# Sparse attention and a dropless mixture of experts: three row gathers one step earlier, a second layer 2 in another PSUM bank, one tile weighed by two engines

## The chip, the cores and the metric

The kernel runs on one core of one Trainium2 chip. The metric is the time of the launch in device microseconds, as a median of several runs. The core has five engines with an instruction stream each: TensorE (PE in the profile, its weight loads PEld), VectorE (DVE), ScalarE (ACT), GpSimd (POOL) and SyncE (SP). They wait for each other by semaphores. Sixteen DMA engines move data; in this kernel SP issues the plain transfers (queue q1) and GpSimd the indirect ones, which take their row numbers from a tile (queue q0).

## The reference

Attention comes first. There are 4 batches, 8 heads, 768 positions and a head dimension of 64. A block of 32 queries sees its own and the neighbouring key blocks, the first and last block, and three sampled blocks; the first and last query blocks see everything. Then each of the 3,072 rows of 512 numbers goes to one of 8 experts:

```python
logits = x @ w_gate
expert_idx = np.argmax(logits, axis=1)
...
for e in range(E):
    lo, hi = (boundaries[e], boundaries[e + 1])
    ...
    h = np.maximum(x_sorted[lo:hi] @ w1[e], 0.0)
    y_sorted[lo:hi] = h @ w2[e]
y = y_sorted[inv_perm]
return (gate_w[:, None] * y).astype(np.float32)
```

w1 is 512 x 1,024 and w2 is 1,024 x 512 for each expert, all in float32; gate_w is the softmax weight of the chosen expert.

## The kernel before

**Attention** is a list of 48 steps (`steps`): four batches, six groups of 128 queries, and two halves of the heads for each. In a step TensorE makes the scores of that step, ScalarE takes their exponential (L361), VectorE masks them (L367), and TensorE multiplies the *previous* step's exponentials with the values (`attend`, L385), in three chunks of the keys. The values that the queries see lie in the tile `around`, in two sets; GpSimd fetches them from `v_rows` with indirect transfers (`fetch_values`, L519), one to three steps ahead. `not_before` (L533) is a copy of one number on GpSimd: it waits for another engine's result, so that the fetches behind it are not issued too soon. In steps of an even place the fetch `fetch_values(b, g, 1, 1)` fills what the third chunk of `attend` reads in the next step. `divide` writes the rows x to `x_rows` in DRAM, `logits` makes their expert scores.

The order of the work on TensorE, VectorE and GpSimd is that of the code (`manual_schedule`); in attention this holds for ScalarE and SP too.

**Routing** is done twice. The rows of the first two batches (A) are sorted while attention still runs on the last two, and fill the first KA = 5 tiles of 128 rows; their row numbers (`gA`) are ready in the fourth-last step. The other tiles (B) are laid out after attention.

**The experts** run over NS = 18 tiles in a loop, with tile i + 1 in layer 1 while tile i is in layer 2. A tile takes these steps:

- `gather(i)` (L1048): GpSimd fetches the tile's 128 rows, 520 numbers each, from `x_rows` into one of four `xg` tiles. Column 512 is gate_w.
- `turn_x(i)`: the rows are transposed, on TensorE (L1119) for tiles 0 to 3 and on VectorE (L1111) after that.
- `layer1(i)` (L1130): two halves g of 16 matmuls each into a PSUM tile `hp`. ScalarE's relu (L1137) empties each half; what is handed in as `between` (the next tile's `turn_x`, or `turn_h`) stands between the halves in TensorE's order.
- `layer2_pe(i)` (L1144): eight matmuls of 512 columns into a PSUM tile of 512 numbers for each partition, which is one bank.
- `weigh(i)` (L1149): ScalarE multiplies the bank with gate_w on its way to SBUF.
- `put` (L1159): GpSimd writes the rows to their places in the output.

Before the loop, tile 0 is turned ahead of attention's last `attend`, and its `layer1` follows with `turn_out_late` (L476) and `turn_x(1)` between the halves.

Three **units** (at tiles 8, 11 and 14, `AT`) take an expert's last two tiles, one of them filled in part, as one wide tile of 128 to 224 columns (`layers_u`, L1248, L1256, L1265), inside a `Switch` over the width. A unit stands together with the layer 2 of two ordinary tiles, i before it and i + 1 behind it. It takes five PSUM banks: `banks[0]` and `banks[1]` from the pool `ps_h`, whose two buffers `layer1` uses also, `banks[2]` and `banks[3]` from the pool `ps_m`, and one from `ps_z`. After a unit comes a **small** tile of 32 rows (`layer1_s` L1198, `turn_h` L1207, `layer2_s` L1215; PSUM from `ps_m`), interleaved with the next tile's `layer1`.

Behind the loop a `Switch` over the number `arm` runs as many further tiles as the data needs beyond NS, with the same `layer1`, `layer2` and `weigh`. SP fetches the expert weights, 2 MB for each layer of a tile, three places ahead into buffers that TensorE has left.

Of the kernel before, what the change touches and what calls it, by code (L numbers as in the profile page):

```python
# [11 lines left out]
AF = mybir.ActivationFunctionType  # L12
# [5 lines left out]
def kernel(  # L18
# [11 lines left out]
    nc = tc.nc  # L30
# [8 lines left out]
    N, DM = out.shape  # L39
# [18 lines left out]
    NS = KA - -(N - KA * P - KU * MW - KS * QS) // P  # L58
# [5 lines left out]
    scale = 1.0 / float(D) ** 0.5  # L64
# [244 lines left out]
    def parity(b, g):  # L309
        return (b * NG + order.index(g)) % 2  # L310
# [220 lines left out]
    def not_before(at):  # L531

        nc.gpsimd.tensor_copy(paced[:], at)  # L533
# [489 lines left out]
    st = [{} for _ in range(NC)]  # L1023
# [22 lines left out]
    def gather(i):  # L1046
        xg = st[i]["xg"] = keep_xg[i % 4]
        nc.gpsimd.indirect_dma_start(  # L1048
            out=xg[:], out_offset=None, in_=x_d[: TA * P, :] if i < KA else x_d[:, :], in_offset=bass.IndirectOffsetOnAxis(ap=of("g", i, P), axis=0),
        )  # L1050
# [91 lines left out]
    def layer2_pe(i, zp):  # L1142
        for fb in range(FB):
            nc.tensor.matmul(  # L1144
                zp[:], lhsT=st[i]["hT"][:, fb, :], rhs=st[i]["w2"][:, fb, :], start=(fb == 0), stop=(fb == FB - 1),
            )

    def weigh(i, zo, zp):
        nc.scalar.activation(zo, zp[:], AF.Copy, scale=st[i]["xg"][:, DM : DM + 1])  # L1149

    def layer2(i, group):
        zp = upper["ps_z"].tile([P, DM], F32, name="zp")
# [157 lines left out]
    for i, (b, g, half) in enumerate(steps):  # L1310
        here = i % (2 * NG)
        prs = (2 * half, 2 * half + 1)
        nxt = steps[i + 2] if i + 2 < len(steps) else None

        if nxt is not None:
            b_, g_, half_ = nxt
            if half_ == 0:
                place_middle(b_, g_)
        if half == 0 and i > 0 and len(tiles_of(g)) > 1:
            if nxt is not None:  # L1320
                not_before(xk[0:1, parity(*nxt[:2]), 0, D : D + 1])
            fetch_values(b, g, 1, 1)
        if nxt is not None and half_ < len(tiles_of(g_)):
            place_keys(b_, g_, half_, on_vector=1 if b_ == B - 1 else NR)
        two = half == 1 and i + 1 < len(steps) and len(tiles_of(steps[i + 1][1])) > 1
        if two:
            b_, g_, _ = steps[i + 1]
            not_before(kr[0:1, parity(b_, g_), 1, 0, NKR - 1 : NKR])
            fetch_values(b_, g_, 1, 0)

        if g == GL:
            plans = [plan_all(b, pr) for pr in prs if b > 0] + [plan_two(b, prs)]
            *e_alls, e = scores(*plans)
            masked_two(e)
            mine = [(b, g, pr, e_alls[pr % 2] if b > 0 else None, e) for pr in prs]
        else:
            found = scores(*[plan(b, g, pr) for pr in prs])
            for e in found:
                masked(e, g)
            mine = [(b, g, pr, None, e) for pr, e in zip(prs, found)]  # L1340
        late = here + 2 * NG * (b - B + 2)
        for what in PARTS.get(late, ()):
            fetch_part(*what)
        if half == 1 and i + 1 < len(steps):
            not_before(mine[1][4][0:1, 0, 0:1])
            fetch_values(*steps[i + 1][:2], 0, 1)

        copy_turned = None
        if b + 1 < B:
            if b == 0 and here < 2:  # L1350
                fill_next(1, 2 * here)
                fill_next(1, 2 * here + 1)
            if 2 <= here < 10:
                copy_turned = turn(b + 1, (here - 2) // 2, here % 2, None, (here - 2) // 2 % 2)
                if here < 6:
                    fill_next(b + 1, here + 2)
        if b + 2 < B and here >= 8:
            fill_next(b + 2, here - 8)

        out_of = steps[i - 3][:2] if i >= 3 and half == 1 else None  # L1360
        if copy_turned:
            copy_turned()
        if i > 0 and before[0][1] != GL:
            attend(before, (lambda: turn_out(*out_of)) if out_of else None)
        elif i > 0:
            for n, (b_, g_, pr, e_all, e) in enumerate(before):
                attend_last(b_, pr, e_all, e)
                if n == 0 and out_of:
                    turn_out(*out_of)
        if "gates" in rt:  # L1370
            gate_weights()
        if out_of:
            logits(*out_of)
            if out_of[1] == order[-1]:
                gate(out_of[0])
        if i > 0:
            divide(*steps[i - 1])
        early(late)
        if half == 0 and nxt is not None:
            if i >= 2:  # L1380
                fetch_ends(*nxt[:2])
                b_, g_, half_ = steps[i - 1]
                not_before(sums[0:1, b_ * NG + g_, 4 * half_ : 4 * half_ + 1])
            fetch_values(*nxt[:2], 0, 0)
        if half == 1 and nxt is not None:
            place_values(*nxt[:2])
        if b + 1 < B:
            load_v(b + 1, V_AT[b > 0].get(here, ()))
            if 7 <= here < 10:
                keep_v(b + 1, (2 * here - 14, 2 * here - 13))  # L1390
        if 3 <= i < 11:
            route_consts(i - 3)
        if i == 11:
            route_tokens()
        if i == len(steps) - 2:
            gather(0)
        if i == len(steps) - 1:
            not_before(mine[1][4][0:1, 0, 0:1])
            gather(1)
        before = mine  # L1400
    turn_x(0)
    attend(before)
    divide(*steps[-1])
    gather(2)
    attn_by_hand.close()
    fetch(2, 1)
    fetch(2, 2)
# [7 lines left out]
    for i in range(NS):  # L1415
        if i == 0:
            ranks("B", TA, NT)
        if i + 3 <= NS + 1:
            gather(i + 3)
        here = AT_S.index(i) if i in AT_S else None  # L1420
        if here is not None:
            layer1_s(here)
            fetch_after(("small", here), 1)
        if i + 1 < NS:
            layer1(i + 1, lambda: turn_x(i + 2), *([turn_h] if here is not None else []))
            fetch_after(i + 1, 1)
        if here is not None:
            layer2_s(here)
            fetch_after(("small", here), 2)

            layer2(i + 1, "rows_out")
            fetch_after(i + 1, 2)
            leave_s(here, "rows_out")
        if i == 0:
            count("B")
            layout_b()
        if i + 3 in AT:
            gather_u(AT.index(i + 3))
        if i + 3 in AT_S:
            gather_s(AT_S.index(i + 3))  # L1440
        if i + 2 in AT:
            turn_u()
        if i + 2 in AT_S:
            turn_s()
        if i in AT or i - 1 in AT:

            continue
        if i + 1 in AT:


            u = AT.index(i + 1)
            zps = [upper["ps_z"].tile([P, DM], F32, name="zp") for _ in range(2)]
            zos = [next_of("z", keep_z) for _ in range(2)]
            banks = [upper["ps_h"].tile([P, DM], F32, name="hpu", tag="hp") for _ in range(2)]
            banks += [upper["ps_m"].tile([P, DM], F32, name="tpu", tag="tpg") for _ in range(2)] + zps[1:]
            layer2_pe(i, zps[0])
            fetch_after(i, 2)
            for more in tc.Switch(index[u], QR // STEP + 1):
                weigh(i, zos[0], zps[0])
                layers_u(u, P + more * STEP, banks)  # L1460
                layer2_pe(i + 1, banks[1])
                weigh(i + 1, zos[1], banks[1])
            fetch_after(("unit", u), 1)
            fetch_after(("unit", u), 2)
            fetch_after(i + 1, 2)
            put(of("s", i, P), zos[0], "rows_out")
            leave_u(u, "rows_out")
            put(of("s", i + 1, P), zos[1], "rows_out")
            continue
        layer2(i, "rows_out")  # L1470
        fetch_after(i, 2)
        if i == 1:
            tokens("B", NT, NB_)
        if i == 2:
            judge()
        if i == 4:
            tokens_s()
        if i == 3:
            for u in range(KU):
                at = rt["xeU"][0:1, KU + u : KU + u + 1]  # L1480
                index[u] = {
                    mybir.EngineType.PE: nc.tensor.value_load(at, min_val=0, max_val=QR // STEP),
                    mybir.EngineType.Activation: nc.scalar.value_load(at, min_val=0, max_val=QR // STEP),
                }
# [93 lines left out]
```

## Time and profile before

| | before |
|---|---|
| median of 3 runs | 640.75 us (636.26 to 643.61) |
| the profiled execution | 641.06 us |
| its span in the profile | 639.4 us |
| TensorE busy | 611.1 us (96%) |
| VectorE, ScalarE, GpSimd busy | 305.4, 230.6, 189.2 us |
| mean granted TensorE clock | 0.973 |
| DMA | 170.94 MB, mean 267 GB/s |

The profile shows one execution. Its page gives the busy time of each engine, the span in 40 slices (PEclk is the granted TensorE clock in tenths, DMA the share of the DMA engines' time), the costliest groups of instructions by line of the kernel, and the transfers. Other views list the instructions of one engine in order of time, the waits by who waited for whom, and the instructions of one tile. A bracket such as [1.75 <-DMA xg<-x_rows,gA] says that the engine sat idle for 1.75 us and that the landing of this transfer ended it. "paced" is what `not_before` writes.

### The profile page before, as it was taken

The numbers are of one execution on the slowest core, as the hardware profiler recorded it, in microseconds if no ns is written. First come the engines' busy times: TensorE is split into PE (matmuls) and PEld (weight loads), VectorE is DVE, ScalarE is ACT, GpSimd is POOL, SyncE is SP. The second block draws the span as 40 slices with busy tenths as digits, with TensorE's granted clock in tenths as the row PEclk, the third lists the DMA queues.
The fourth block names the chain that finished last, engine by engine and source line by source line (L and its number), as shares of the span: only waits on it lengthen the run. The fifth ranks groups of instructions, "written<-read, shape, count | busy, mean of one in ns | idle before, by whom it ended". The sixth has DMA issues, their size and how long they took to land. (4 is left out here: it accounts for less than half of the span.)

```text
span 639.4 us, 21377 instructions
## 1 busy us (share of the span) xinstructions
PE 611.1 (96%) x8938; PEld 512.6 (80%) x8938; DVE 305.4 (48%) x980; ACT 230.6 (36%) x456; POOL 189.2 (30%) x289
## 2 busy tenths in 40 slices
PE   7998989999999999989999999999999999999994
PEld 7898888889998989987777777877878787966862
DVE  7546665765578647725952485303091208303300
ACT  5546755774577758721111011111111111111110
POOL 2245844552366336720112221011401140020110
PEclk8869999997999989999999999999999999999998
DMA  8889977896797748899988999879997999669710
GB/s 266 210 182 233 238 195 165 205 244 180 162 209 202 240 141 260 261 344 339 345 306 315 336 387 351 289 234 385 397 399 281 370 398 399 260 220 408 281 39 19
DMA packets 125066, 170.94 MB, mean 267 GB/s; under 512 B 71236, under 2 KB 71237, under 8 KB 124934
## 3 DMA queue, kind: packets, MB, share of 16 engines
q1 hardware_dynamic: 114896, 137.61, 66.2%
q0 software_dynamic: 10000, 31.59, 15.9%
q8 instruction: 80, 1.31, 0.9%
q14 instruction: 52, 0.43, 0.2%
q10 hardware_dynamic: 38, 0.00, 0.0%
HBM read 150.11 MB, written 19.33 MB: 265 GB/s over the span
## 5 line engine op out<-in xcount | busy, mean ns | idle before, releaser
L1111 DVE STREAM_TRANSPOSE around<-xg 32x128 f32<-32x128 f32 x240 | 72.6, 303 | 121.9 <-PE hp L1130 92.7
L519 POOL DMA_INDIRECT around<-v_rows,rows_of x88 | 99.7, 1133 | 59.3 <-issue 23.4
L361 ACT ACTIVATE ea<-s 128x768 f32<-128x768 f32 x104 | 79.8, 809 | 78.4 <-PE s L356 66.7
L1130 PEld LDWEIGHTS hp<-around,room 128*128 128x128 f32 x832 | 94.5, 192 | 4.3 <-issue 2.7
L385 PE MATMUL op<-around,ea 128*64 128x65 f32 x2112 | 90.5, 229 | 7.3 <-DMA around<-v_rows,rows_of 6.1
L1130 PE MATMUL hp<-around,room 128*128 128x128 f32 x832 | 96.4, 276 | 0.9 <-ACT kr L1137 0.9
L385 PEld LDWEIGHTS op<-around,ea 128*64 128x64 f32 x2112 | 78.8, 141 | 16.1 <-DMA around<-v_rows,rows_of 7.4
L367 DVE TENSOR_TENSOR ea<-ea,mask 128x768 f32<-128x768 f32 x80 | 73.2, 954 | 20.0 <-ACT ea L361 19.1
L1144 PE MATMUL zp<-room,kr 128*128 128x512 f32 x176 | 77.6, 594 | 0.0
L1137 ACT ACTIVATE kr<-hp 128x512 f32<-128x512 f32 x36 | 21.5, 597 | 117.1 <-PE hp L1130 109.1
L1144 PEld LDWEIGHTS zp<-room,kr 128*128 128x128 f32 x176 | 32.6, 190 | 37.2 <-issue 37.2
L1159 POOL DMA_INDIRECT out_dram<-kr,sB x14 | 14.1, 1008 | 161.3 <-ACT kr L1149 106.0
L1149 ACT ACTIVATE kr<-zp,xg 128x512 f32<-128x512 f32 x16 | 11.0, 687 | 101.2 <-PE zp L1144 101.2
L1130 PEld LDWEIGHTS hp<-around,other 128*128 128x128 f32 x384 | 43.8, 192 | 3.0 <-issue 2.3
L1130 PE MATMUL hp<-around,other 128*128 128x128 f32 x384 | 44.4, 276 | 0.5 <-ACT kr L1137 0.5
L1237 DVE STREAM_TRANSPOSE ea<-ea 32x128 f32<-32x128 f32 x84 | 21.7, 285 | 32.6 <-DMA ea<-x_rows,gB 31.9
L1144 PE MATMUL zp<-other,kr 128*128 128x512 f32 x80 | 35.3, 593 | 0.0
L1144 PEld LDWEIGHTS zp<-other,kr 128*128 128x128 f32 x80 | 14.9, 190 | 17.4 <-issue 17.4
L356 PE MATMUL s<-other,kr 64*128 64x64 f32 x352 | 27.0, 266 | 1.2 <-issue 1.2
L356 PE MATMUL s<-room,kr 64*128 64x64 f32 x352 | 26.7, 266 | 0.5 <-issue 0.5
L1159 POOL DMA_INDIRECT out_dram<-kr,sA x5 | 5.1, 1024 | 73.9 <-ACT kr L1149 73.9
L356 PEld LDWEIGHTS s<-other,kr 64*128 64x128 f32 x352 | 25.3, 195 | 1.2 <-issue 1.2
(362 smaller groups left out, 945.0 us busy)
## 6 DMA issues: line engine op xcount, KB each, us to landing
room<-in_moe_w_dram SPq DMA_DIRECT2D x30, 2048.0 KB
other<-in_moe_w_dram SPq DMA_DIRECT2D x16, 2048.0 KB
room<-in_moe_w_dram SPq DMA_DIRECT2D x16, 512.0 KB
x_rows<-xb SPq DMA_DIRECT2D x20, 256.0 KB
room<-in_k_dram SPq DMA_DIRECT2D x24, 192.0 KB
room<-in_q_dram SPq DMA_DIRECT2D x24, 192.0 KB
v_rows<-room SPq DMA_DIRECT2D x12, 260.0 KB
v_rows<-other SPq DMA_DIRECT2D x12, 260.0 KB
```

What stands on the lines that cost most here:

```text
L356: nc.tensor.matmul(s[:, hh, a : a + n], lhsT=keys(r), rhs=queries(r), start=True, stop=True)
L361: nc.scalar.activation(e, s[:, :, : 6 * D], AF.Exp, scale=scale)
L367: nc.vector.tensor_tensor(e, e, m[:, None, :].to_broadcast([P, 2, 6 * D]), op=ALU.mult)
L385: nc.tensor.matmul(op[ti * D : (ti + 1) * D, pr % 2, hh, : D + 1], lhsT=e, rhs=values[:, (2 * pr + hh) * VW : (2 * pr + hh + 1) * VW], sta ...
L519: nc.gpsimd.indirect_dma_start(out=around[p0:, par, 1 + ti + 2 * ch, :], out_offset=None, in_=v_d[b][:, :], in_offset=bass.IndirectOffsetO ...
L1111: nc.vector.transpose(xT[d, :, t], xg[t, :DM].rearrange("p (c q) -> p c q", c=DB)[:, :, d])
L1130: nc.tensor.matmul(hp[:, m, :], lhsT=st[i]["w1"][:, c, fb * P : (fb + 1) * P], rhs=st[i]["xT"][:, c, :], start=(c == 0), stop=(c == DB - 1),)
L1137: nc.scalar.activation(hT[:, g * (FB // 2) : (g + 1) * (FB // 2), :], hp[:], AF.Relu)
L1144: nc.tensor.matmul(zp[:], lhsT=st[i]["hT"][:, fb, :], rhs=st[i]["w2"][:, fb, :], start=(fb == 0), stop=(fb == FB - 1),)
L1149: nc.scalar.activation(zo, zp[:], AF.Copy, scale=st[i]["xg"][:, DM : DM + 1])
L1159: ins = nc.gpsimd.indirect_dma_start(out=to[:, :], out_offset=bass.IndirectOffsetOnAxis(ap=at, axis=0), in_=rows, in_offset=None, bounds_c ...
L1237: nc.vector.transpose(xT_u[d, :, j * P + tq * 32 : j * P + (tq + 1) * 32], xg_u[t, j, :DM].rearrange("p (c q) -> p c q", c=DB)[:, :, d],)
```

## The change

Three edits.

1. gather(0), gather(1) and gather(2) are issued at the ends of attention's last three steps, in place of the ends of the last two and the place behind the last `divide`. The `not_before` of the last step now stands ahead of gather(2), where it stood ahead of gather(1).
2. Inside a unit, the layer 2 of tile i + 1 goes to `banks[3]`, from the pool `ps_m`, in place of `banks[1]`, from `ps_h`.
3. For tile NS - 1 = 17, `weigh` is cut into two halves of 256 columns: VectorE takes the upper, ScalarE the lower one. Every other tile's `weigh` stays as it was.

```diff
     def weigh(i, zo, zp):
-        nc.scalar.activation(zo, zp[:], AF.Copy, scale=st[i]["xg"][:, DM : DM + 1])
+        of_i = st[i]["xg"][:, DM : DM + 1]
+        if i == NS - 1:
+            nc.vector.tensor_scalar_mul(zo[:, DM // 2 :], zp[:, DM // 2 :], of_i)
+            nc.scalar.activation(zo[:, : DM // 2], zp[:, : DM // 2], AF.Copy, scale=of_i)
+            return
+        nc.scalar.activation(zo, zp[:], AF.Copy, scale=of_i)
...
             route_tokens()
-        if i == len(steps) - 2:
-            gather(0)
-        if i == len(steps) - 1:
-            not_before(mine[1][4][0:1, 0, 0:1])
-            gather(1)
+        if i >= len(steps) - 3:
+            if i == len(steps) - 1:
+                not_before(mine[1][4][0:1, 0, 0:1])
+            gather(i - len(steps) + 3)
         before = mine
     turn_x(0)
     attend(before)
     divide(*steps[-1])
-    gather(2)
     attn_by_hand.close()
...
                 layers_u(u, P + more * STEP, banks)
-                layer2_pe(i + 1, banks[1])
-                weigh(i + 1, zos[1], banks[1])
+                layer2_pe(i + 1, banks[3])
+                weigh(i + 1, zos[1], banks[3])
```

## The prediction

> **What bounds it now.** I read the page first, then TensorE's order of time where the change sits, then the waits. The page:
>
> ```profile
> span 639.4 us, 21377 instructions
> PE 611.1 (96%) x8938; PEld 512.6 (80%) x8938; DVE 305.4 (48%) x980; ACT 230.6 (36%) x456; POOL 189.2 (30%) x289
> PEclk8869999997999989999999999999999999999998
> ```
>
> TensorE is busy for 611.1 of 639.4 us. The page's chain of waits holds only the last 1.3 us (the last write's issue), so it doesn't lead back into the kernel; TensorE's own gaps do, and I added them up from the matmuls' starts and ends: 18.6 us in all before the last matmul, most of it in attention. A change that neither cuts matmuls nor moves the clock can win only such a gap, or the tail behind the last matmul. From 240 us to the tail the stretches at half clock are over (table of windows: PEclk 1.00 in each), so a gap that closes there is worth its own length.
>
> Two kinds of gap lie under this change. The first is where attention ends; TensorE in order of time, the bracket telling an idle time and what ended it:
>
> ```profile
> 274.72 1.35 PE L385 MATMUL op<-around,ea 128*64 128x65 f32 x31
> ...
> 276.47 0.66 PE L1119 MATMUL tp<-ident,xg 128*128 128x128 f32 x4
> 277.06 1.62 PE L385 MATMUL op<-around,ea 128*64 128x65 f32 x48
> 278.61 3.84 PE L1130 MATMUL hp<-around,room 128*128 128x128 f32 x32
> 282.29 0.60 PE L476 MATMUL xrl<-ident,xb 128*128 128x128 f32 x4
> 284.63 0.66 PE L1119 MATMUL tpg<-ident,xg 128*128 128x128 f32 x4 [1.75 <-DMA xg<-x_rows,gA]
> ```
>
> Tile 1's transpose (L1119) waits 1.75 us for gather(1). GpSimd's order tells why it is late:
>
> ```profile
> 268.38 0.98 POOL L519 DMA_INDIRECT around<-v_rows,rows_of  x1 [0.16 <-issue]
> 269.67 0.95 POOL L519 DMA_INDIRECT around<-v_rows,rows_of  x1 [0.30 <-issue]
> 270.93 1.00 POOL L1048 DMA_INDIRECT xg<-x_rows,gA  x1 [0.31 <-issue]
> 275.83 0.18 POOL L533 COPY paced<-ea 1x1 f32<-1x1 f32 x1 [3.90 <-DVE ea L367]
> 276.49 0.97 POOL L1048 DMA_INDIRECT xg<-x_rows,gA  x1 [0.48 <-issue]
> ```
>
> gather(1) stands behind not_before (L533), held until VectorE has masked the last step; its issue at 276.49 lands at 284.59.
>
> The second kind is behind each unit. TensorE after the first one, and the same wait summed over the run in the view of waits (total, times, longest):
>
> ```profile
> 437.37 0.38 PE L1207 MATMUL tps__7960<-ident,ea 128*128 128x128 f32 x2
> 438.22 3.84 PE L1130 MATMUL hp<-around,other 128*128 128x128 f32 x32 [0.47 <-ACT kr L1137]
> ```
>
> ```profile
> PE hp L1130 <- ACT kr L1137: 1.4, 3, 0.5
> ```
>
> The second half of layer1 starts only when ScalarE's relu has emptied the first half. In the built program both halves lie in the same PSUM bank there: the unit's second layer 2 held the other one.
>
> **Part 1, the gathers.** Nothing is added or removed; on GpSimd gather(0) moves ahead of the last values' fetch (L519, at 269.67), gather(1) directly behind that fetch and ahead of not_before, gather(2) behind not_before; gather(3) moves up a place. SP's order does not change.
>
> The gain: gather(1) is then the third in the row 269.67, 270.93, about 272.2. The transfer now issued at 270.93 landed at 276.06, 5.1 us on; the slowest one of this stretch took 8.1 us. So gather(1) lands at 277.3, at worst 280.3, and tile 1's transpose is due at 282.9: the 1.75 us go.
>
> The loss: the last fetch gets gather(0)'s place. Behind it on GpSimd stand only gathers; TensorE's attend waits for it with its third chunk. Single matmuls of that attend are at 275.30 and then at 275.45, where the spacing is 0.05, and the fetch's last piece landed at 275.40: it is just in time today. Fetch and gather are equal in size (128 rows of 2,080 bytes), so the two swap landings: the fetch at 276.06, attend 0.65 us later. Bounds: 0 (most of its 16 pieces came 1.1 us ahead of the last one, which may be another engine's luck), and 3.6, if it took the slow 8.1 us from 270.93 (279.0). I take 0.65: the row is the same slot of the same queue, while the 8.1 us belong to a gather issued just behind a 2 MB weight load (275.70) that has no like at 271.
>
> The Trainium skill would have it otherwise: "DMA: Bandwidth & Descriptors", the section on the anatomy of one DMA on the GpSimd path, gives about 2.0 us plus bytes/436e3, here 2.6 us (an estimate). By it the fetch lands at 273.5, ahead of its need, and the part is worth the whole 1.75. The rows say 5 to 8 us, because 0.86 to 1.03 of DMA time is taken (windows from 250 to 275); they decide. Sum: -1.75 + 0.65 = **-1.10 us**.
>
> What is late next: tile 1's weights (issued 273.88 and 275.10, landed by 280.4, needed about 287.6), tile 2's gather (gather(1)'s old place, landed 284.6, needed at 293.0 - 1.1). The gathers put 0.27 MB each ahead of those weights, 0.75 us at the 355 GB/s of 270 to 274; the slack is 7 us. The routing on VectorE starts from the last logits on TensorE (288.8), so it moves up with them.
>
> **Part 2, the bank.** layer2_pe(i+1) writes banks[3] (ps_m) in place of banks[1] (ps_h). What it must wait for in banks[3], ScalarE's copy of the fourth quarter of zT, the transposes before it wait for anyway: no new wait. In the built program the next layer1's halves then lie in two banks, and the second half has no wait on ScalarE left. turn_h moves into layer1_s's bank, whose reader (L1202) it waits for as its own input. What comes next, layer2_s, needs turn_h's copy (438.44) and would start at 441.5: no wait. Three units: 3 x 0.47 = **-1.41 us**. From below: 0 if a wait takes its place. I take the whole, since the wait is the one the trace names, three times of equal length.
>
> **Part 3, the split weigh.** Which tile is it? Rows of weigh, from the view of tile xg:
>
> ```profile
> L1149 ACT ACTIVATE kr<-zp,xg x16: 687/687/688, 304.2 to 631.3; 128x512 f32<-128x512 f32 x16
> L1149 ACT ACTIVATE kr<-hpu,xg x3: 687/688/688, 431.9 to 570.2; 128x512 f32<-128x512 f32 x3
> ```
>
> 16 + 3 = 19 tiles run, and NS is 18: the tile at the end (631.3) is number 18, in the arm behind the main loop. The split is made for i == 17, here:
>
> ```profile
> 617.34 0.69 ACT L1149 ACTIVATE kr<-zp,xg 128x512 f32<-128x512 f32 x1 [6.23 <-PE zp L1144]
> 620.94 0.60 ACT L1137 ACTIVATE kr<-hp 128x512 f32<-128x512 f32 x1 [2.92 <-PE hp L1130]
> ```
>
> Nor do the halves run together: in the built program ScalarE's half waits on VectorE's. The skill's page "PSUM — Partial Sum Buffer" (on bank collisions) speaks against the idea: two engines in one bank and quadrant at a time are not arbitrated, they raise an error, so accesses have to take turns. VectorE's half: 692 ns for 512 columns (L1135) and 166 for 8 (L490) give 425 for 256; ScalarE's: 385 for 256 (L1202) plus the 90 that the scale costs (687 less 597, L1149 and L1137) give 475. In turn, with 50 ns for the hand-over, 0.95 us against 0.69: +0.26; side by side it would be -0.21. No run here shows the pair. I take +0.26, off the path: it delays tile 17's write, and ScalarE's jump into the last arm by 0.5, so L1137 goes from 620.94 to 621.4 and ends at 622.0; TensorE reads it at 624.2. Cover 2.2 us, cost **0**; without that cover at most 0.5. VectorE has nothing more to do in that arm.
>
> **Sum.** -1.10 - 1.41 + 0 = -2.5 us. The profiled execution took 641.06 (span 639.4 and 1.7 around it): 638.55. The median shown is 640.75, which would give 638.2. I say **638.4**. The three runs lie 7 us apart, three times the effect, and stretches of half clock in attention (PEclk digits under 9, 31 us in all by the clock record) are what could differ between them; about 1% (6.4 us) is what a measurement of this kernel can tell from no change.
>
> **Rivals.**
> 1. The fetch is late by much (the slower side). Place: attend's third chunk at 275.3. With the 8.1 us that a gather took at 276.5 it comes 3.6 us late: -2.5 - 0.65 + 3.6 = +0.4, 641.5. It decides once it lands after 278.6. For: the queue is full, 1.03 in the window 270 to 274. Against: the four transfers issued from 266.6 to 270.9 all landed within 6.5 us. Chance 0.07.
> 2. The gathers bring nothing, since the delay of the fetch eats the gap: -1.41, 639.65. It needs the fetch at 277.2. Chance 0.12.
> 3. The change doesn't do what it says in the units: another wait replaces the 0.47. Then -1.10, 639.95. For: nothing but that the old wait was short; against: the built program. Chance 0.06.
> 4. The fetch costs nothing, because its last piece comes earlier: -3.2, 637.9. Chance 0.15.
> 5. Another number of half-clock stretches: a stretch of 6.8 us costs 3.4. It has nothing to do with the change and goes either way, 635 or 642. Chance 0.10 that it hides the rest.
> The forecast itself: 0.50.
>
> **Range.** Cases 1 to 4 span 637.9 to 641.5; case 5 and the spread of the runs widen it: 634.5 to 642.0. Faster by over 1% needs 634.3, out of reach of the gaps touched here without the clock's help: 0.07. Slower by over 1% needs 647: 0.06. Within 1%: 0.87.
>
> **What would show it.** Right: no idle time before tile 1's L1119 near 283.5; L385's third chunk waiting 0.5 to 1 us for the fetch near 275.3 to 276; no wait of L1130 on L1137 after the units; tile 17 with a VectorE row of about 425 ns, then a ScalarE row of about 475, and tile 18 with 687. Wrong: a wait of over 1.7 us in L385 there, new waits of L1207 or L1215, tile 17's halves overlapping, or a difference that lies in attention before 265 us.

## The result and the profile after

The change as made took **634.86 us** (median; 628.11 to 639.7) against 637.37 us (632.81 to 647.42) for the kernel before, measured with it. The ratio is **0.9943** (95% interval 0.9918 to 0.9968), or -3.6 us (-5.2 to -2.0). It is taken over fast runs alone (a slow one is over 1.5% above the fastest of its kernel), so its -3.6 us are not the difference of the two medians, -2.5. The forecast had the right sign and the right mechanism, and two thirds of the size: -2.5 us. Repeats on three other chips gave 0.998, 1.0004 and 0.999: there most of the gain was lost, for a reason that the prediction had put aside. The experiments find it.

The profiled execution after took 632.85 us. Its page, beside that of before:

```profile
span 631.1 us, 21379 instructions
PE 605.5 (96%) x8938; PEld 507.8 (80%) x8938; DVE 305.9 (48%) x981; ACT 230.0 (36%) x456; POOL 191.5 (30%) x289
PEclk8799999999899999999999999999999999999998
```

The two spans differ by 8.3 us, and half of that isn't the change's. Subtracting the starts of the same instructions in TensorE's order gives -4.0 us before 265 us, where both programs are alike. Then the difference moves in four places only: by -1.97 at tile 1's transpose (-1.91 at its first matmul, the rest at its second), and by -0.73 behind each of the three units (-0.63 at the first matmul behind the wait, -0.10 at the second). The change is -4.2 us in this pair.

Where attention ends, TensorE in order of time (start, duration, engine, line; a bracket would tell an idle time):

```profile
272.45 0.66 PE L1119 MATMUL tp<-ident,xg 128*128 128x128 f32 x4
273.04 1.62 PE L385 MATMUL op<-around,ea 128*64 128x65 f32 x48
274.59 3.84 PE L1130 MATMUL hp<-around,room 128*128 128x128 f32 x32
278.27 0.60 PE L476 MATMUL xrl<-ident,xb 128*128 128x128 f32 x4
278.70 0.60 PE L1119 MATMUL tpg<-ident,xg 128*128 128x128 f32 x4
```

No bracket is left: from L476 to tile 1's L1119 it is 0.43 us, where it was 2.34. GpSimd shows the new order:

```profile
264.08 0.98 POOL L519 DMA_INDIRECT around<-v_rows,rows_of  x1 [0.54 <-PE xr L486]
265.36 0.95 POOL L1048 DMA_INDIRECT xg<-x_rows,gA  x1 [0.31 <-issue]
266.62 1.31 POOL L519 DMA_INDIRECT around<-v_rows,rows_of  x1 [0.30 <-issue]
268.23 0.94 POOL L1048 DMA_INDIRECT xg<-x_rows,gA  x1 [0.30 <-issue]
271.83 0.18 POOL L533 COPY paced<-ea 1x1 f32<-1x1 f32 x1 [2.66 <-DVE ea L367]
```

gather(1), at 268.23, is now ahead of `not_before`. The last fetch (266.62) stands behind gather(0) and is no later against TensorE than it was: its last piece landed at 271.38, where it was 275.40, and TensorE's work there is 4.02 us earlier too. Behind a unit:

```profile
431.37 0.38 PE L1212 MATMUL tps__7960<-ident,ea 128*128 128x128 f32 x2
431.58 3.74 PE L1130 MATMUL hp<-around,other 128*128 128x128 f32 x32
```

From the second `turn_h` matmul to layer1's second half it is 0.11 us; it was 0.74 around the gap of 0.47. The matmul after that follows in 0.11 us, where it took 0.21 behind the wait. And the split tile, then the last one:

```profile
609.25 0.48 DVE L1151 TENSOR_SCALAR kr<-zp,xg 128x256 f32<-128x256 f32 x1 [12.96 <-PE zp L1144]
609.77 0.47 ACT L1152 ACTIVATE kr<-zp,xg 128x256 f32<-128x256 f32 x1 [6.87 <-DVE kr L1151]
623.15 0.69 ACT L1154 ACTIVATE kr<-zp,xg 128x512 f32<-128x512 f32 x1 [6.26 <-PE zp L1144]
```

ScalarE's half starts when VectorE's has ended, and tile 18 at the end is still weighed by ScalarE alone, as forecast.

### The profile page after: what moved, and what is told of

The parts are those of the page before. It is cut to its first block, busy times and chain, and to the rows that moved or that the text cites. A ratio compares the mean times of both kernels' runs of the same rounds, so it can differ in the third digit from the quotient of the medians.

```text
span 631.1 us, 21379 instructions
## 1 busy us (share of the span) xinstructions
PE 605.5 (96%) x8938; PEld 507.8 (80%) x8938; DVE 305.9 (48%) x981; ACT 230.0 (36%) x456; POOL 191.5 (30%) x289
## 5 line engine op out<-in xcount | busy, mean ns | idle before, releaser
L385 PE MATMUL op<-around,ea 128*64 128x65 f32 x2112 | 87.9, 225 | 9.4 <-DMA around<-v_rows,rows_of 6.8
L1130 PEld LDWEIGHTS hp<-around,room 128*128 128x128 f32 x832 | 94.5, 192 | 2.9 <-issue 2.7
L1130 PE MATMUL hp<-around,room 128*128 128x128 f32 x832 | 96.2, 276 | 0.0
L385 PEld LDWEIGHTS op<-around,ea 128*64 128x64 f32 x2112 | 75.9, 137 | 18.6 <-DMA around<-v_rows,rows_of 7.9
L1137 ACT ACTIVATE kr<-hp 128x512 f32<-128x512 f32 x36 | 21.5, 597 | 114.4 <-PE hp L1130 103.2
L1130 PEld LDWEIGHTS hp<-around,other 128*128 128x128 f32 x384 | 43.8, 192 | 2.3 <-issue 2.3
L1130 PE MATMUL hp<-around,other 128*128 128x128 f32 x384 | 44.3, 275 | 0.0
L1242 DVE STREAM_TRANSPOSE ea<-ea 32x128 f32<-32x128 f32 x84 | 21.7, 285 | 32.3 <-DMA ea<-x_rows,gB 31.7
L351 PE MATMUL s<-room 64*64 64x64 f32 x736 | 24.7, 247 | 0.3 <-DVE room L157 0.3
```

The costliest lines, as they stand in the source:

```text
L351: nc.tensor.matmul(s[j * D : (j + 1) * D, hh, a : a + n], lhsT=keys(r), rhs=queries(r), start=True, stop=True)
L385: nc.tensor.matmul(op[ti * D : (ti + 1) * D, pr % 2, hh, : D + 1], lhsT=e, rhs=values[:, (2 * pr + hh) * VW : (2 * pr + hh + 1) * VW], sta ...
L1130: nc.tensor.matmul(hp[:, m, :], lhsT=st[i]["w1"][:, c, fb * P : (fb + 1) * P], rhs=st[i]["xT"][:, c, :], start=(c == 0), stop=(c == DB - 1),)
L1137: nc.scalar.activation(hT[:, g * (FB // 2) : (g + 1) * (FB // 2), :], hp[:], AF.Relu)
L1242: nc.vector.transpose(xT_u[d, :, j * P + tq * 32 : j * P + (tq + 1) * 32], xg_u[t, j, :DM].rearrange("p (c q) -> p c q", c=DB)[:, :, d],)
```

## The experiments

### One part at a time: e1, e2, e3

e1 has the new order of the gathers alone, e2 the bank alone, e3 the split of tile 17 alone; each is the matching hunk of the diff above.

> The gathers' move alone. Theory A (a closed wait is worth its idle time and the restart of the array, about 0.16 us more; the last values' fetch is behind one gather now, but lands in time when the queue runs ahead): from L476's start to tile 1's L1119 it takes 0.43 us where it took 2.34 before, -1.9 us; the third chunk of the second-last attend waits 0 to 0.7; the whole is 1.2 to 1.9 us faster, ratio 0.997 to 0.998. Theory B (the prediction's sum): the fetch costs 0.65 each time and the wait is worth 1.75, so -1.1 us, ratio 0.998. Theory C (the gathers' move is what the measured 3.6 us come from, the bank nothing): -3.6 us, ratio 0.994.

> The bank of the unit's second layer 2 alone. Theory A: behind each unit the second half of layer1 starts 0.11 us after the last turn_h matmul where it started 0.74 after it: 3 x 0.63 = -1.9 us, ratio 0.997. Theory B (the prediction's sum): 3 x 0.47 = -1.4 us, ratio 0.998. Theory C: no difference, because a wait on another engine takes its place. Tile 1's wait of 1.75 us stays in all of them.

> The split of tile 17's weigh alone. Theory A and B: its halves run one after the other, 0.48 on VectorE and 0.47 on ScalarE, about 1.0 us in place of 0.69; it lies off the path, TensorE's order of time from tile 17 to tile 18 does not change, ratio 1.000. Theory D (it is part of the gain or of a loss): a difference of over 0.3 us in TensorE's time between tile 17's and tile 18's layer 2.

| | ratio, 95% interval | us |
|---|---|---|
| e1 gathers | 0.9957 (0.9925 to 0.9989) | -2.7 |
| e2 bank | 0.9984 (0.9954 to 1.0014) | -1.0 |
| e3 split | 1.0013 (0.9984 to 1.0043) | +0.8 |

Only e1 is clear of 1. e1 and e2 add up to -3.7 us beside the change's -3.6, but e2's part alone is not shown by its time (its half-clock time, explained under e9, is 2.3 ± 1.5 us above before's, which could hide 1.2 us). For the bank the traces decide: in e2's profile every unit has its 0.11 us, three times 0.73 less, and tile 1's wait is still there and longer than in before. e3 is nothing that can be told from zero. e1's profile shows the last fetch paid for:

```profile
281.31 0.66 PE L1119 MATMUL tpg<-ident,xg 128*128 128x128 f32 x4 [2.92 <-DMA xg<-x_rows,gA]
```

```profile
275.14 0.62 PE L385 MATMUL op<-around,ea 128*64 128x65 f32 x13 [0.51 <-DMA around<-v_rows,rows_of]
```

The first line is e2's, the second e1's. So the wait at tile 1 is no constant: 1.75 us in before, 2.92 here, 1.96 in e3 and 2.36 in e6 below, with the same order of gathers. The price of the fetch varies too: 0.84 us in e1 (from the second-last `attend`'s L468 to tile 0's turn 2.93 us, 2.09 where nothing is late), 0.22 in the change, 0.25 in before and 0.70 in e2, which has before's order.

### Where the gathers stand: e4, e5

e4 puts gather(0) and gather(1) both behind the last fetch; e5 both ahead of it.

```diff
         if i == len(steps) - 2:
             gather(0)
+            gather(1)
         if i == len(steps) - 1:
             not_before(mine[1][4][0:1, 0, 0:1])
-            gather(1)
+            gather(2)
...
-    gather(2)
```

> gather(0) and gather(1) both behind the last values' fetch and ahead of not_before, gather(2) behind it; nothing is put ahead of the fetch. Theory A: tile 1's wait goes (0.43 us from L476 to L1119), the third chunk of the second-last attend waits no more than before (0.1): -1.9 us, and no measurable difference from the gathers' move as it was made, whose fetch is mostly in time. Theory B: 0.65 us faster than that move, because the fetch is not put off. In both, gather(0) lands before tile 0's turn needs it.

> gather(0) and gather(1) both ahead of the last values' fetch. Theory A: each transfer ahead of the fetch puts its landing off by about 0.65 us, if the queue is what limits it; with two ahead it lands 1.3 us later than in the kernel before, 1.9 to 2.6 us after the turn_out of that step, and from that turn_out (L468) to tile 0's turn it takes 2.09 + 0.9 to 1.6, so 3.0 to 3.7 us. Tile 1's wait is gone (0.44 from L476 to L1119). Theory E (the queue runs ahead, the fetch's place in it does not matter): 2.1 to 2.4 us.

e4: 0.9958 (0.9928 to 0.9988), the same as e1. So the fetch's lost place costs too little to be measured, and what counts is gather(1) ahead of `not_before`. e5 took 641.69 us in its one run; two places lost do show:

```profile
276.44 0.62 PE L385 MATMUL op<-around,ea 128*64 128x65 f32 x13 [1.65 <-DMA around<-v_rows,rows_of]
```

This is the prediction's first rival, one place further on: 1.65 us of TensorE in place of the 1.75 removed.

### The wait made longer, and filled: e9, e10

e9 is before with gather(1) and gather(2) swapped behind `not_before`, so that tile 1's rows come one place later. e10 is before with 16 transposes of the identity (nobody reads them) ahead of tile 1's turn, so that TensorE works through part of the wait.

```diff
-            gather(1)
+            gather(2)
...
-    gather(2)
+    gather(1)
```

```diff
+    def filler():
+        fill = upper["ps_z"].tile([P, DM], F32, name="fill", tag="zp")
+        for _ in range(16):
+            nc.tensor.transpose(fill[:, :P], ident[:], ident[:])
...
-    layer1(0, lambda: turn_out_late(*steps[-1][:2]), lambda: turn_x(1))
+    layer1(0, lambda: turn_out_late(*steps[-1][:2]), filler, lambda: turn_x(1))
```

> The kernel before, with gather(1) and gather(2) changed in their places behind not_before: gather(1) is issued 1.3 us later. Theory K (a wait of TensorE's over about half of a 3.4 us stretch of the clock's record is followed by a stretch at half clock, which costs 1.6 us more): tile 1's wait grows from 1.75 to 2.9 us as seen so far to 3.2 to 4.4 us, and a half-clock stretch of 3.4 us or more follows it between 280 and 295 us: +1.4 us by the wait and up to +1.6 by the clock, ratio 1.002 to 1.005. Theory A (a wait costs itself and 0.16 us): +1.4 us, ratio 1.002, and no half-clock stretch behind it.

> The kernel before, with 16 transposes of the identity in TensorE's order ahead of tile 1's turn, where it waits for gather(1): 1.8 us of work that nobody reads, in a wait that cost 1.9 us and more. The wait for the gather stays as it is. Theory K: TensorE has no long idle time there, so no half-clock stretch follows between 280 and 295 us; against the kernel before that is 0 in executions that had none, and -1.6 us in those that had one: ratio 0.998 to 1.000. Theory A: ratio 1.000, and half-clock stretches there as often as before, since they have another cause (two of three profiles with the wait had one).

e9: 1.0068 (1.0039 to 1.0097), +4.3 us, over three times the 1.3 us of one place in the queue. Its profile shows where more goes, in the wait and in the window behind it (window, length, busy time of PE, PEld, DVE, ACT, POOL, then PEclk, DMA share, GB/s):

```profile
284.01 0.66 PE L1119 MATMUL tpg<-ident,xg 128*128 128x128 f32 x4 [2.71 <-DMA xg<-x_rows,gA]
```

```profile
281.50:284.90 3.40, 0.89 (x8) 0.89 (x9) 0.00 (x0) 0.67 (x2) 0.00 (x0) 1.00 1.03 417
284.90:288.30 3.40, 3.40 (x18) 3.40 (x18) 0.00 (x0) 0.39 (x1) 0.00 (x0) 0.51 1.03 398
```

TensorE is idle for 2.5 us of the first window; in the next 3.4 us it runs at half clock (0.51): 16 matmuls start there, 0.21 us apart, where 30 would at 0.11. That is another 1.6 us. The clock record changes in steps of 3.41 us, and here a wait that fills most of one such window is followed by one at half clock. So were e2's wait of 2.92 us and e3's of 1.96. In the profile of before the 1.75 us were cut in two by a window's edge (1.34 and 0.43), in e6 the 2.36 (1.85 in one window), and none followed: luck. Over all of e9's runs the time at half clock, 2 x (1 - mean clock) x time, is 26.7 us against before's 21.4, difference 5.3 ± 1.7 (standard error), so 2.6 us of its 4.3. e10 came out at 1.0005 (0.9976 to 1.0034), at 19.6 us of half clock (-1.7 ± 1.6): this says only that filling is no gain.

### The split at the end, and another bank: e6, e8

e6 is before with the split for tile 18 (`if i >= NS`), where the weighing is on the path. e8 is before with `banks[2]` in place of `banks[1]`.

> The kernel before, with the split of weigh for the tiles behind the main loop in place of tile 17: tile 18, the last one that runs, is weighed by both engines. If the halves take turns: from the last matmul's start to the last write's issue 1.64 + 0.95 - 0.69 = 1.9 us, so +0.3 us at the very end. If they run side by side: 1.64 - 0.2 = 1.4 us. Tile 1's wait stays, and with it (theory K) a half-clock stretch in some executions.

> The bank alone, with banks[2] in place of banks[3]. If what counts is only that the second layer 2 leaves ps_h's second buffer free, then as e2: 0.11 us from turn_h's last matmul to layer1's second half behind each unit, against 0.74 before, and no new wait at layer 2 itself. The rival, that banks[3] is special since its reader is done longest, expects a wait of layer 2 or of turn_h behind ScalarE's copy, some tenths of a us, three times.

e6 took 646.74 us in one run. From the last matmul to `put` it is 2.07 us, 1.64 before: the split costs **0.43 us**: 0.31 since the halves take turns (1.00 us in place of 0.69), and 0.13 since VectorE starts 0.81 us behind the last matmul's start and ScalarE alone 0.68.

```profile
636.38 0.48 DVE L1151 TENSOR_SCALAR kr<-zp,xg 128x256 f32<-128x256 f32 x1 [27.02 <-PE zp L1144]
636.90 0.47 ACT L1152 ACTIVATE kr<-zp,xg 128x256 f32<-128x256 f32 x1 [6.91 <-DVE kr L1151]
```

e8 (647.49 us, one run) has 0.11 us behind each unit like e2: `banks[2]` does as well as `banks[3]`.

### On other chips: e11, e7, e12

The medians of before up to here were 637.37, 638.79 and 639.44 us. The next chip drawn ran before in 648.47. e11 is e4 and the bank (no split), a candidate better than the change. e7 is e11 with tile 18's layer 2 in two banks of 256 columns each, so that only half is left to weigh after the last matmul. e12 is the change as made.

```diff
+        if i >= NS:
+            for part in range(2):
+                zp = upper["ps_z"].tile([P, DM], F32, name="zp")
+                d = slice(part * DM // 2, (part + 1) * DM // 2)
...
+                nc.scalar.activation(zo[:, d], zp[:, : DM // 2], AF.Copy, scale=st[i]["xg"][:, DM : DM + 1])
```

> Gathers of tiles 0 and 1 both behind the last values' fetch, banks[3] for the second layer 2, tile 17 weighed by ScalarE alone. The parts add up: gathers behind the fetch measured 0.9958 (-2.7 us), the bank 3 x 0.63 = 1.9 us by the traces, so 0.993 (0.990 to 0.996), -4.6 us. Against the change as made (0.9943): the fetch keeps its slot, so tile 0's turn comes 2.1 us behind the last xr copy (2.3 to 2.9 with the fetch one place later), worth 0.2 to 0.8 us or 0.999 of it. The rival, that the parts share one gain (the clock), expects no better than 0.9955. In the profile: no idle time at tile 1's L1119 nor at L385 there, 0.11 us from turn_h to layer1's second half.

> As e11, and tile 18's layer 2 computed as two 256-column halves in two banks, each weighed by ScalarE alone, the first half under the second half's matmuls. If it is the shared bank that makes a split of the weighing useless, then the halves don't take turns here: about 475 ns behind the last matmul in place of 687, -0.2 us at the end, 0.9997 of e11 (not to be told from 1). The rival, that the write (put) waits on something else, expects 1.64 us from last matmul to put as before.

> The change as made, once more, beside e11 on the same chip. Expected 0.9943 (0.992 to 0.997) as in its first measurement, and behind e11 by 0 to 0.8 us. The profile tells what another execution pays at the last fetch (L385's idle: 0.2 to 0.8 us expected) and whether the stretch 275 to 295 us holds a piece at half clock: none expected, since no idle of over 1.3 us is left in it.

e11 1.0027 (0.9999 to 1.0055), e7 1.0002 (0.9974 to 1.003), e12 0.998 (0.9956 to 1.0004). All three expectations of a gain failed, though every wait that should be gone is gone: 0.11 us at the units, 0.44 at tile 1's turn, no idle time for the last fetch. (e7's tail did what was expected: from the last matmul to `put` 1.16 us in place of 1.64, for 0.24 us more of matmuls, so -0.24; no measurement here resolves that.)

### An offset, or the chip: e13 to e16

e13 is before against itself, e14 the change as made, e15 is e11 and e16 is e4, once more. They fell on another such chip, before 648.48 us.

> The kernel before, unchanged, against itself: what the measurement shows where nothing differs. Expected 1.000; the intervals given are about 0.003 to each side, so within that if they hold all that varies. If a ratio carries an offset beyond its interval, up to 0.005 here. Its profile adds one more execution of tile 1's wait: 1.75 to 2.9 us of idle time at L1119 if attention runs as in the first executions; about 0.2 if it runs some 8 us behind, as on the third chip.

> The change as made. If the gain is that of the waits (1.9 us at the units, 1.2 to 2.4 us at the end of attention), 0.993 to 0.9955 wherever attention runs as in the first executions; 0.995 to 0.998 where it runs some 8 us behind and tile 1's wait is hidden. If the offset theory holds, anything from 0.992 to 1.000.

> Gathers of tiles 0 and 1 both behind the last fetch, banks[3], tile 17 not split. By the waits 0 to 0.8 us better than the change as made: 0.992 to 0.9955 (0.994 to 0.998 on a late attention). If 1.0027 of the last measurement belongs to this kernel itself, over 1.000 again, and its attention up to 265 us longer than that of the others in the profile.

> The gathers behind the last fetch alone, banks[1], no split. By the waits 1.9 us more than e15 (0.003 of it) and 0.995 to 0.997 against before (0.997 to 0.999 on a late attention). On an offset its place relative to e15 is open.

e13 0.9986 (0.9957 to 1.0015), e14 1.0004 (0.9979 to 1.0029), e15 0.9998 (0.9973 to 1.0022), e16 1.0042 (1.0018 to 1.0065). The kernel before against itself is 1 within its interval, so it is no offset. e16, which as e4 gained 2.7 us on a chip of the first kind, loses 2.7 here.

What takes the gain back is on record for every run, the granted clock (half-clock time as above, in us, over the runs that the ratio uses):

| on a chip near 648 us | half clock, this | before | difference |
|---|---|---|---|
| e11 | 29.5 | 21.7 | +7.8 ± 1.7 |
| e7 | 25.5 | 21.7 | +3.8 ± 1.6 |
| e12 as made | 25.4 | 21.7 | +3.6 ± 1.5 |
| e13 before | 20.1 | 21.8 | -1.6 ± 1.9 |
| e14 as made | 30.3 | 21.8 | +8.6 ± 1.6 |
| e15 | 26.5 | 21.8 | +4.8 ± 1.4 |
| e16 | 29.4 | 21.8 | +7.6 ± 1.5 |

With TensorE busy, half of such a difference is lost: 2 to 4 us. On the chip of e1 and e4 these differ by +0.6 ± 1.5 and 0.0 ± 1.9. The profiles show the place. TensorE in e13, then in e14, while GpSimd issues the last fetches:

```profile
270.39 1.26 PE L385 MATMUL op<-around,ea 128*64 128x65 f32 x34
271.97 0.37 PE L385 MATMUL op<-around,ea 128*64 128x65 f32 x5 [0.31 <-issue]
272.74 0.28 PE L385 MATMUL op<-around,ea 128*64 128x65 f32 x2 [0.40 <-issue]
273.46 0.46 PE L385 MATMUL op<-around,ea 128*64 128x65 f32 x7 [0.44 <-issue]
```

```profile
271.61 0.73 PE L385 MATMUL op<-around,ea 128*64 128x65 f32 x7
272.74 0.22 PE L385 MATMUL op<-around,ea 128*64 128x65 f32 x1 [0.41 <-issue]
273.45 0.37 PE L385 MATMUL op<-around,ea 128*64 128x65 f32 x5 [0.49 <-issue]
274.91 2.23 PE L385 MATMUL op<-around,ea 128*64 128x65 f32 x35 [1.08 <-issue]
```

"issue" means that nothing the profile shows was waited for. These stops are the mark of such a chip: 22 to 29 of over 0.1 us in attention, where the first chips' profiles have 6 to 9. Between 63 and 76% of their time lies within the indirect issues on GpSimd shifted by 1 us, which cover 36 to 38% of attention (both from 65 us on). e14's GpSimd:

```profile
269.18 0.98 POOL L519 DMA_INDIRECT around<-v_rows,rows_of  x1 [0.54 <-PE xr L486]
270.46 0.95 POOL L1048 DMA_INDIRECT xg<-x_rows,gA  x1 [0.31 <-issue]
271.72 0.95 POOL L519 DMA_INDIRECT around<-v_rows,rows_of  x1 [0.30 <-issue]
272.97 0.95 POOL L1048 DMA_INDIRECT xg<-x_rows,gA  x1 [0.30 <-issue]
```

Four indirect issues in an unbroken row; before has three. The stops end about 1 us behind the row's end, and each issue more keeps them on. Then comes the clock: e14's record is at half from 274.0 to 284.2. The first two of these windows beside the one ahead (columns as above):

```profile
270.60:274.00 3.40, 2.01 (x20) 1.29 (x20) 0.00 (x0) 0.00 (x0) 2.71 (x3) 1.00 1.01 327
274.00:277.40 3.40, 2.49 (x47) 2.38 (x51) 1.58 (x2) 1.51 (x2) 0.00 (x0) 0.50 0.59 212
277.40:280.80 3.40, 3.40 (x56) 3.25 (x48) 1.10 (x5) 0.81 (x1) 0.00 (x0) 0.50 0.37 88
```

### The row broken: e17, e18

If the row is what costs, it can be kept at three: gather(0) behind the last fetch as before, and gather(1) held until VectorE has masked step 46. e17 is e11 with this; e18 is the change as made beside it. The chip was again one of the second kind (before 649.4 us).

```diff
         if i == len(steps) - 2:
             gather(0)
+            not_before(mine[1][4][0:1, 0, 0:1])
             gather(1)
```

> gather(0) behind the last fetch as before, gather(1) behind a wait for step 46's mask, gather(2) behind that for step 47's; banks[3]; tile 17 not split. If the length of the row costs, then on a chip with a base near 648 us its clock stays at before's (0.982) and it gains the waits: 0.993 to 0.996. If the row has nothing to do with it, it lies where e11 and e15 lay there (0.9998 and 1.0027). On a chip with a base near 639 us both expect 0.993 to 0.996. gather(1) is then issued about 3 us behind gather(0) and lands 5 to 8 us later, still ahead of tile 1's turn: no idle time at L1119, unless it takes over 9 us.

> The change as made beside it. On a chip with a base near 648 us: 0.998 to 1.000 with a mean clock some 0.003 to 0.006 under before's, as on two such chips; near 639 us: 0.994 to 0.997 at before's clock.

e17 **0.9955** (0.9919 to 0.9991), half clock -1.2 ± 1.9; e18 0.999 (0.9955 to 1.0024), +5.7 ± 2.2. Both came as the row theory said. The two intervals overlap, but compared with each other, on one chip, e17 is 2.7 ± 1.2 us faster than e18 (standard error) with 6.9 ± 2.4 us less half-clock time. GpSimd and TensorE in e17 (the bracket of the copy names another VectorE instruction; the row itself reads the mask's `ea`):

```profile
267.80 0.98 POOL L519 DMA_INDIRECT around<-v_rows,rows_of  x1 [0.54 <-PE xr L486]
269.08 0.95 POOL L519 DMA_INDIRECT around<-v_rows,rows_of  x1 [0.30 <-issue]
270.34 0.95 POOL L1048 DMA_INDIRECT xg<-x_rows,gA  x1 [0.30 <-issue]
274.97 0.18 POOL L533 COPY paced<-ea 1x1 f32<-1x1 f32 x1 [3.69 <-DVE sums L446]
275.63 0.97 POOL L1048 DMA_INDIRECT xg<-x_rows,gA  x1 [0.48 <-issue]
```

```profile
271.34 0.22 PE L385 MATMUL op<-around,ea 128*64 128x65 f32 x1 [0.37 <-issue]
272.05 1.44 PE L385 MATMUL op<-around,ea 128*64 128x65 f32 x41 [0.49 <-issue]
```

gather(1) at 275.63 is early enough: no idle time at tile 1's turn. e17 is the best version measured on this kind of chip; on the first kind it wasn't run. The ten profiles from chips of this kind, by the length of the row:

| row | profiles | TensorE's stops there, us | half clock begins within 1 us of their end |
|---|---|---|---|
| 3 | e8, e13, e17 | 1.34, 1.15, 1.19 | in e8 |
| 4 | e7, e11, e12, e14, e15, e16, e18 | 2.06, 2.34, 2.03, 2.30, 2.25, 2.23, 2.57 | in all but e18 |

The groups don't touch: a fourth issue costs 1.0 us of stops, and the clock behind. The row behind the last `not_before` counts too: with three gathers (e8, e13) it is 7.3 us from tile 0's turn to L476, with two 6.4 to 6.8, and 5.8 on the first chips with either (7.4 in e5, with a half-clock window in it). So part of tile 1's wait is hidden on this kind of chip. In e13, with before's order, it is

```profile
287.13 0.66 PE L1119 MATMUL tpg<-ident,xg 128*128 128x128 f32 x4 [0.54 <-DMA xg<-x_rows,gA]
```

and 0.21 us in e8. From tile 0's turn to tile 1's it takes 8.5 and 8.1 us in these two, 6.8 to 7.3 in the seven with a row of four and in e17: the gathers' move has 0.9 to 1.7 us to gain here, where it had 1.9.

## Where the prediction failed, and what was right in it

**Two steps failed.** One is "a gap that closes there is worth its own length", with the +0.65 for the last fetch beside it: the terms -1.75, -1.41 and +0.65 measured -1.97, -2.20 and 0 in the pair of traces, -4.2 us in place of -2.5. The total alone doesn't show this, since its interval takes in -2.5; the traces do. The other is "about 1% (6.4 us) is what a measurement of this kernel can tell from no change", by which the forecast change could not have been seen. The intervals measured are 0.23 to 0.36% to each side, and -0.57% is clear of no change.

**The mechanism: right.** The wait of L1119 on gather(1), the wait of L1130 on L1137, the tile that is split and its halves in turn all came as worked out, and no other wait of TensorE took their place.

**The term -1.41 for the bank: too small.** It measured 3 x 0.73 = -2.20. The trace models a matmul's end: a start to end time of 0.27 us stands where the next one starts 0.11 us on, so 0.16 us of each idle time is hidden in the drawn end of the matmul before. And behind the wait the second matmul starts 0.21 us after the first, 0.10 later than elsewhere. The true cost of a wait is the spacing of starts with it less that without it, over the first few matmuls. By this tile 1's 1.75 is 1.97.

**The term +0.65 for the last fetch: too large.** The fetch is one place later on GpSimd, but the queue's own position against TensorE moves by as much from one execution to the next: 0.22 us paid in the change and 0.25 in before, 0.84 in e1, and 0.70 in e2, which has before's order. e4, with the fetch's place kept, measures like e1. The wait of L385 that was forecast came in e1 (0.51 us), not in the change. The prediction took one execution's landing times for a fixed schedule.

**The term -1.75 for tile 1: one draw.** The same wait was 2.92, 2.36 and 1.96 us in other profiles. With the 0.22 added, the mean of the four is 2.5 us, which e1's -2.7 fits.

**"From 240 us to the tail the stretches at half clock are over", and rival 5, "It has nothing to do with the change": wrong**, and the larger error. It held in the execution shown. A wait of the size removed here can bring a stretch at half clock by itself (e9, e2, e3), and on the second kind of chip the change's own row of four issues brings one, which takes 2 to 4 us back. The Trainium skill ("TensorE: Matmul & The Clock Gate", the sections "What's actually happening" and "HAM oscillation") judges activity by a free-running window of 3.4 us, as the record here does, but lets the clock fall after a whole idle window and warns of gaps of more than 3.4 us. By that rule none of the waits touched here could move the clock. Here 2.5 us of idle time in a window (e9) were enough; the measurement decides.

**The price of a busy queue: right.** The Trainium skill ("DMA: Bandwidth & Descriptors", the anatomy of one DMA on the GpSimd path) gave an estimate of 2.6 us for a gather; in the row ahead of `not_before` the change's gathers landed 5.35 and 4.46 us after issue, the two behind it 8.05 and 8.72.

**The split at zero: right** (behind the third unit TensorE's starts in before and after move apart no further), and its price where it isn't hidden was under-estimated: +0.43 in e6 against +0.26, since VectorE's half took 484 ns and not 425 (ScalarE's 475, the hand-over 40), and VectorE starts 0.13 us later behind the last matmul than ScalarE does. `put` follows the last of them in 0.27 us with one engine or two.

**Open.** What TensorE waits for in the stops of the second kind of chip isn't named by the trace. That the row of issues sets their length is shown by e17 and the table; through which resource is not. Nor is it shown why two kinds of chip differ. Each chip was measured at one time only, the three of the second kind after the three of the first, so that the difference could also lie in the time and not in the chip.

## What to carry to other kernels

Take a wait's size from several executions, and its cost from the spacing of starts with and without it, over the first few matmuls behind it. A move of DMAs on GpSimd's queue is also a change of how many issues follow each other without a break: look at what TensorE does during that row and just behind it, and break the row where the data isn't due yet. Compare the mean granted clock over all runs of the two kernels before a missing gain is looked for among the waits.

## What was not expected of the hardware

- The clock record's windows of 3.41 us can be set against TensorE's idle time in each (as drawn, all 20 profiles, from 60 us on). All ten windows at full clock with 1.95 us or more of idle time were followed by one at half clock, none of the 3,202 with 0.90 us or less, and 21 of the 61 between. A window at half clock costs 1.6 us where TensorE is the bound (e9).
- On chips where this kernel takes 648 us instead of 639, TensorE stops 22 to 29 times in attention with no cause shown, mostly about 1 us behind the indirect issues of GpSimd; a row of four makes 2.0 to 2.6 us of stops, a row of three 1.2 to 1.3.
- The two halves of a bank, read by two engines, ran in turn, because in this program one waits for the other: 484 + 475 ns and 40 between (e6), against 687 by one engine. VectorE's first half also started 0.13 us later behind the matmul.
